# Pre-norm attention and GEGLU block on one core: first steps on token chunk 0, and ScalarE's extra work spaced by a backlog count

## The chip, the cores and the metric

The kernel runs on one core of a Trainium2 chip. The metric is the device time of one execution in microseconds (us). PE is TensorE (PEld its weight loads), DVE is VectorE, ACT is ScalarE, POOL is GpSimd and SP is SyncE, which issues the DMAs.

## The reference

```python
B, S, D, H, F = 1, 2048, 512, 32, 1792           # bf16, Dh = 16
def attn(x):                                      # wqkv: D x 3D, wo: D x D
    q, k, v = split_heads(x @ wqkv)
    p = softmax(einsum("bhqd,bhkd->bhqk", q, k) * Dh ** -0.5)
    return merge_heads(einsum("bhqk,bhkd->bhqd", p, v)) @ wo
def ffn(x):
    return (gelu_tanh(x @ w_gate) * (x @ w_up)) @ w_down
h  = x + attn(layernorm(x))                       # no scale or shift, eps 1e-5
h2 = h + ffn(layernorm(h))                        # the result
```

## The kernel before

**Planner.** The Python code walks through the whole program and appends instructions to one list per engine (PE, ACT, DVE, POOL, SP) with `P.op` and `P.dma`. It derives the semaphore waits from the buffers that each reads and writes. Every engine works off its list strictly in order, so an instruction that waits holds up all that was appended to the same engine behind it. This also goes for SP: its DMAs wait in line.

**Start (lines 327 to 388).** The 2048 tokens are 16 tiles of 128, or 4 chunks of 512. DMAs load `x_sb` by chunks, then `wqkv_sb` in one piece, then `wo_sb`. `ln1_stats(c)` takes mean and variance of a chunk's tiles on DVE (lines 351, 352), and POOL turns them into `rstd` and `nmr1` with a power (lines 355 to 358). `ln1_norm` writes the normalized `xn_sb` on DVE for chunks 0 to 2 and on POOL for chunk 3 (line 362); PE transposes each tile with four matmuls (line 367), and ACT copies the result from PSUM to `xnT` (line 369). `w_order` reorders the K and Q weights on DVE (line 374). Then `dense.run_items(5)` projects K for all four chunks and Q for chunk 0 of the first head group (`item_projT`, line 564); ACT writes them with their masks straight from PSUM (`direct`, lines 591 and 593).

**Heads.** Eight slots of four heads each; a head has 16 channels in a 32-row strip. One K or Q projection (`ht`) gives two slots: the even one by a masked copy, and the odd one from a copy `QKS` which a DMA shifts by 16 partitions into one of two `QKS2` buffers (line 597), which POOL then masks (`mask_emit`, lines 584 and 586). `qk_late` holds the copies of the five first projections, whose shifts come just ahead of step 0.

**Steps (loop at the end, "ticks").** The queries are 8 groups (`gi`) of 256; a unit is one group and one slot, 64 units of 16 steps, 1024 steps. In each step pass 1 computes two score tiles (line 666) of 512 keys, and DVE takes their row maxima (`TENSOR_REDUCE`, line 675). POOL combines them, SP transposes them by DMA (line 715), and POOL adds them to Q (line 720). Pass 2 follows 24 steps later: PE computes the transposed scores with the maximum subtracted (line 736, two tiles a step), and ACT takes two exponentials of 128 x 512 (line 748) into a ring `PTM`, `PTE`, `PTG`. The four PSUM banks 4 to 7 hold pass 2's tiles and one item of the dense stream.

**Dense stream.** `Dense` is a queue of generators. A call of `dense.piece()` emits some four matmuls, and each step calls it once; before pass 2 has begun, twice. Items: K, Q and V projections (`item_projT`, `item_projV`, line 616), `item_pv` (probabilities times V, line 762, evacuated into `OA`), `item_ofin` (transposes, evacuated into `OAT`), `item_oproj` (ACT sums `xres` and squares it into `OnT`, lines 875 and 882), `item_gate` and `item_up` (line 942, evacuated into `g_sb` and `u_sb`), `item_down` (line 990). Where a step has less than two pieces, `dummy` fills it with matmuls that nobody reads (line 1148). `startable` says whether the item at the head may begin.

**ScalarE's extras.** `evac_act` (line 529) is ACT's copy out of PSUM. The tanh of the GELU (line 925, in `gelu_chain.later`) and the squares (line 882, `sq`) are put off by a step while the set `act_extra` holds this step or the one before:

```python
if not force[0] and (dense.now in act_extra or (n < 3 and (dense.now - 1) in act_extra)):
    defer(1, lambda: later(n + 1))
    return
act_extra.add(dense.now)
```

The evacuations of gate, up, OA, OAT and the projections do not ask.

**End.** Behind the last step pass 2 runs out, and the last group's output projection, layer norm and feed-forward follow (`tail_b`). With `gi` the index of a query group, the last one is `GL` = 7; it uses ACT's own GELU (line 955).

## Time and profile before

| what | value |
|---|---|
| median of 3 runs (lowest, highest) | 1288.84 us (1288.76, 1289.89) |
| the profiled execution's own time | 1289.83 us |
| its span, first to last instruction | 1287.7 us |
| busy: PE, DVE, ACT, POOL | 91%, 94%, 93%, 59% |
| DVE row maxima (line 675) | 1024, busy 1174.2 us |
| ACT exponentials (line 748) | 1388 + 420 + 240 |
| HBM over the span | 11 GB/s |

Lines of the profile name source line, engine, operation, tile written and tiles read, and shapes; then the count, the busy time, the mean length of one, and the idle time before them with what ended it. Instructions on one engine overlap a little, so the distance of two starts can be shorter than the length of one.

### The profile page before, as it was taken

How to read it: one execution, taken by the hardware profiler on the slowest of the kernel's cores; microseconds unless marked ns; L12 is line 12 of the kernel's file. 1: busy time of each engine (PE TensorE's matmuls, PEld its weight loads, DVE VectorE, ACT ScalarE, POOL GpSimd, SP SyncE). 2: the span in 40 equal slices, each digit the busy share in tenths (PEclk: the TensorE clock that was granted, in tenths of full speed). 3: DMA queues.
4: the chain of work that ended last, by engine and by line, in shares of the span. 5: the costliest groups of instructions: out<-in, count | busy, mean ns of one | idle time of the engine just before them, and what ended most of it. 6: DMA issues, size and time to landing. Idle time of an engine off the chain costs nothing.

```text
span 1287.7 us, 31480 instructions
## 1 busy us (share of the span) xinstructions
PE 1175.5 (91%) x12702; PEld 411.7 (32%) x12702; DVE 1205.1 (94%) x1104; ACT 1201.3 (93%) x2438; POOL 759.9 (59%) x1523
## 2 busy tenths in 40 slices
PE   3999988899999999999999999989999999999998
PEld 2222222233323332233323333233322333233335
DVE  5899999999999999999999999999999999999913
ACT  3599999999999999999999999999999999999992
POOL 5567763477635774467733876367744777347840
PEclk9999999999999999999999999999999999999999
DMA  3110003300010000100001000100001000100000
GB/s 131 42 32 23 21 20 118 88 6 5 4 30 13 6 4 9 29 11 3 6 22 20 6 6 5 28 14 6 6 8 34 5 4 6 30 14 4 5 12 17
DMA packets 48688, 27.45 MB, mean 21 GB/s; under 512 B 34976, under 2 KB 47008, under 8 KB 48544
## 3 DMA queue, kind: packets, MB, share of 16 engines
q1 hardware_dynamic: 48544, 25.44, 7.6%
q8 instruction: 101, 1.65, 0.5%
q14 instruction: 43, 0.35, 0.1%
HBM read 11.80 MB, written 2.10 MB: 11 GB/s over the span
## 4 chain that ended last, share of the span: by engine, by line
ACT 48%; PE 37%; DVE 11%; issue 2%; POOL 0%; DMA 0%
ACT PTM L748 27%; PE pbank L762 10%; DVE PM L675 10%; ACT PTG L748 8%; PE pbank L1148 6%; PE pbank L666 6%; PE pbank L736 5%; ACT PTE L748 5%; PE pbank L990 5%; ACT th_sb L925 2%; ACT g_sb L529 1%; PE pbank L616 1%; ACT OA L529 1%; ACT u_sb L529 1%; PE pbank L564 1%
## 5 line engine op out<-in xcount | busy, mean ns | idle before, releaser
L675 DVE TENSOR_REDUCE PM<-pbank 128x2 f32<-128x1024 f32 x1024 | 1174.2, 1215 | 29.8 <-PE pbank L666 14.1
L748 ACT ACTIVATE PTM<-pbank 128x512 bf16<-128x512 f32 x1388 | 741.9, 655 | 17.8 <-PE pbank L736 8.4
L736 PE MATMUL pbank<-QT,KT 32*128 32x256 bf16 x4096 | 492.2, 273 | 3.4
L666 PE MATMUL pbank<-KT,QT 32*128 32x512 bf16 x2048 | 397.6, 384 | 9.5 <-DVE PM L675 5.4
L1148 PE MATMUL pbank<-ones_bf,ident 128*128 128x512 bf16 x846 | 261.5, 384 | 39.9 <-ACT u_sb L529 8.3
L748 ACT ACTIVATE PTG<-pbank 128x512 bf16<-128x512 f32 x420 | 228.8, 645 | 4.2 <-PE pbank L736 1.9
L666 PEld LDWEIGHTS pbank<-KT,QT 32*128 32x128 bf16 x2048 | 97.6, 91 | 346.8 <-DVE PM L675 135.9
L736 PEld LDWEIGHTS pbank<-QT,KT 32*128 32x128 bf16 x4096 | 165.2, 92 | 53.6 <-ACT PTM L748 22.2
L762 PE MATMUL pbank<-PTM,VA 128*17 128x256 bf16 x2776 | 154.9, 275 | 14.9 <-PE pbank L762 0.2
L748 ACT ACTIVATE PTE<-pbank 128x512 bf16<-128x512 f32 x240 | 137.4, 653 | 3.1 <-PE pbank L736 1.4
L701 POOL TENSOR_TENSOR MX<-PM,MX 128x8 f32<-128x8 f32 x64 | 12.9, 201 | 170.2 <-DVE PM L675 170.2
L1148 PEld LDWEIGHTS pbank<-ones_bf,ident 128*128 128x128 bf16 x846 | 51.5, 97 | 151.3 <-ACT PTM L748 90.7
L797 POOL TENSOR_TENSOR LINV<-OAT,negone 128x16 f32<-128x16 f32 (+1 forms) x32 | 92.7, 2898 | 7.6 <-DVE OAT L518 7.6
L762 PEld LDWEIGHTS pbank<-PTM,VA 128*17 128x17 bf16 x2776 | 42.7, 87 | 107.5 <-PE pbank L762 75.6
L942 PE MATMUL pbank<-hnT_l,wu_sb 128*128 128x256 bf16 x448 | 67.1, 275 | 5.0 <-ACT PTG L748 0.2
L942 PE MATMUL pbank<-hnT_l,wg_sb 128*128 128x256 bf16 x448 | 67.0, 275 | 4.3 <-ACT PTG L748 0.6
L690 POOL TENSOR_TENSOR MX<-PM,MX 128x8 f32<-128x8 f32 x64 | 13.0, 204 | 97.5 <-DVE PM L675 97.5
L934 POOL TENSOR_TENSOR th_sb<-th_sb,g_sb 128x512 f32<-128x512 f32 x49 | 62.2, 1269 | 4.1
L931 POOL TENSOR_TENSOR th_sb<-th_sb,g_sb 128x512 f32<-128x512 f32 x49 | 62.1, 1267 | 2.9
L983 POOL TENSOR_TENSOR GUT<-th_sb,u_sb 128x512 bf16<-128x512 f32 x49 | 62.2, 1268 | 2.7
L990 PE MATMUL pbank<-wd_sb,GUT 128*128 128x512 bf16 x224 | 60.5, 382 | 3.5
L720 POOL TENSOR_TENSOR QT<-QT,STG 128x256 bf16<-128x256 bf16 x64 | 42.8, 669 | 34.0 <-DMA STG<-ST 33.9
(128 smaller groups left out, 1069.9 us busy)
## 6 DMA issues: line engine op xcount, KB each, us to landing
QKS<-QKS SPq DMA_DIRECT2D x32, 112.0 KB, 2.1
x_sb<-in_A_x_dram SPq DMA_DIRECT2D x4, 512.0 KB, 5.5
xres<-in_A_x_dram SPq DMA_DIRECT2D x16, 128.0 KB, 2.2
out_dram<-out_sb SPq DMA_DIRECT2D x16, 128.0 KB, 1.7
wg_sb<-in_B_w_gate_dram SPq DMA_DIRECT2D x4, 448.0 KB, 4.9
wu_sb<-in_B_w_up_dram SPq DMA_DIRECT2D x4, 448.0 KB, 4.8
wqkv_sb<-in_A_wqkv_dram SPq DMA_DIRECT2D x1, 1536.0 KB, 10.3
wd_sb<-in_B_w_down_dram SPq DMA_DIRECT2D x3, 512.0 KB, 6.5
```

Of the source, the lines that this page charges most:

```text
L666: P.op("pe", lambda e, g=g, b=b: e.matmul(pbank[:, b, :], QT[32 * g:32 * g + 32, c, slot, 128 * qt:128 * qt + 128], KT[32 * g:32 * g + 32, ...
L675: P.op("dve", lambda e: e.tensor_reduce(out=PM[:, par, qt, kc, g:g + 2], in_=pbank[:, b:b + 2, :], axis=AX.X, op=ALU.max), reads=[("pb", b ...
L736: P.op("pe", lambda e, kt=kt, i=i: e.matmul(pbank[:, b, 256 * i:256 * i + 256], KT[32 * g:32 * g + 32, slot, 128 * kt:128 * kt + 128], QT[ ...
L748: P.op("act", lambda e, b=b, pi=pi: e.activation(out=PTt(pi), in_=pbank[:, b, :], func=ACT.Exp), reads=[("pb", b)], writes=[("PT", pi)], e ...
L762: P.op("pe", lambda e, g=g, kt=kt, pi=pi, i=i: e.matmul(pbank[32 * g:32 * g + 17, b, 0:256], VA[:, kt, 4 * slot + g, :], PTt(pi)[:, 256 * ...
L797: P.op("pool", lambda e: e.tensor_tensor(out=li, in0=oat4[:, :, :, 16], in1=negone[:, 0:8 * ns].rearrange("p (q h) -> p q h", q=2), op=ALU ...
L931: o(1.27, lambda e: e.tensor_tensor(out=ts_, in0=ts_, in1=gs, op=ALU.mult), [("th", par), ("g", par)])], then=done)
L934: o(1.27, lambda e: e.tensor_tensor(out=ts_, in0=ts_, in1=gs, op=ALU.mult), [("th", par), ("g", par)])], then=lambda: defer(TANH_LAG, lamb ...
L942: P.op("pe", lambda e, dc=dc, fc=fc, i=i: e.matmul(pbank[:, b, 256 * i:256 * i + 256], w[:, dc, 128 * fc:128 * fc + 128], hT[:, dc, :], st ...
L983: P.op("pool", lambda e: e.tensor_tensor(out=o_ap, in0=shp(ts_), in1=shp(us), op=ALU.mult), reads=[("th", par), ("u", par)], writes=o_keys ...
L990: P.op("pe", lambda e: e.matmul(pbank[:, b, :], GUT[:, fc, 128 * k:128 * k + 128], wd_sb[:, fc, :], start=(fc == 0), stop=False), reads=[( ...
L1148: P.op("pe", lambda e: e.matmul(pbank[:, b, :], ident[:], ones_bf[:, 0:512], start=True, stop=True), reads=["ident", "ones_bf"], writes=[( ...
```

## The change

- **Start.** The K and Q weights are loaded as a piece of their own ahead of V's. The layer norm is done tile by tile: statistics on DVE (`stats_dve`) or on ACT (`stats_act`: a copy and a square, each with an accumulated sum; tiles 4 to 6, 11 and 14). Chunk 0 is transposed on PE as before; the tiles of chunks 1 to 3 are transposed by DMAs on SP (`xnT_dma`). The weights are reordered by head group, the first on DVE, the others on ACT beside the steps. Only K and Q of chunk 0 are projected ahead of step 0. The norm of chunk 3, its transposes, the statistics of tiles 12 to 15 and the other K chunks of the first head group come at given steps (`early`) or as items of the dense stream; those K items write their even slot at once (`at_once`).
- **Steps before pass 2.** The second `dense.piece()` is left out in every fourth step. `dummy` takes a bank that the current item does not use.
- **Warm-up.** 16 and 3 filler matmuls at the start (`warm`).
- **Spacing.** The set `act_extra` becomes a number, `act_lag`. Each extra adds its cost in us, and each step takes off 1.135 less 0.478 per exponential. Tanh and squares wait while it is above 0.2 (tanh: plus 0.1 for each step that it has waited). Gate and up items start only at 0.4 or below. A gate item starts only when its buffer is free or the next item with a set time is at least 10 steps off; the first down item of a group starts only when the group's products are all issued, instead of waiting 7 steps with the bank in hand.
- **End.** The choice of the GELU goes by `gi == GL`.

The diff, cut to its core:

```diff
+LAG_START = 0.4
+LAG_OP = 0.2
...
-        P.dma("sp", lambda e: e.dma_start(out=wqkv_sb[:], in_=wv), "wqkv", writes=["wqkv"])
+        P.dma("sp", lambda e: e.dma_start(out=wqkv_sb[:, :, 0:2 * D], in_=wv[:, :, 0:2 * D]), "wqk", writes=["wqk"])
+        P.dma("sp", lambda e: e.dma_start(out=wqkv_sb[:, :, 2 * D:3 * D], in_=wv[:, :, 2 * D:3 * D]), "wqkv", writes=["wqkv"])
...
-        ln1_stats(0)
-        ln1_stats(1)
-        ln1_norm(0, "dve")
-        ln1_stats(2)
-        ln1_norm(1, "dve")
-        ln1_stats(3)
-        ln1_norm(2, "dve")
-        w_order(wk_r, D, "wk_r")
-        ln1_norm(3, "pool")
-        w_order(wq_r, 0, "wq_r")
...
+        def xnT_dma(t):
+            P.dma("sp", lambda e: e.dma_start_transpose(out=xnT[:, :, 128 * t:128 * t + 128], in_=xn_sb[:, t, :]), ("xnT", t), reads=[("xn", t)], writes=[("xnT", t)])
...
+        def warm(n):
+            for _ in range(n):
+                P.op("pe", lambda e: e.matmul(pbank[:, 0, :], ident[:], ones_bf[:, 0:512], start=True, stop=True), reads=["ident", "ones_bf"], writes=[("pb", 0)], sig=False)
+
+        warm(16)
+        for t in range(4):
+            stats_dve(t)
+        rstd_bn(0, 4)
+        rstd_pow(0, 4)
+        for t in range(4, 7):
+            stats_act(t)
+        stats_dve(7)
+        stats_dve(8)
+        rstd_sums(4, 7)
+        rstd_bn(7, 8)
+        rstd_pow(4, 8)
+        for t in range(4):
+            norm1(t, "dve")
+            xnT_pe(t, 4 + t)
+        warm(3)
+        stats_dve(9)
+        w_order("k", 0, "dve")
+        w_order("q", 0, "dve")
+        stats_act(11)
+        stats_dve(10)
+        rstd_bn(8, 11)
+        rstd_sums(11, 12)
+        rstd_pow(8, 12)
+        nmr(8, 12)
+        for t in range(8, 12):
+            norm1(t, "pool")
+
+        def c3_rest():
+            rstd_bn(12, 14)
+            rstd_sums(14, 15)
+            rstd_bn(15, 16)
+            rstd_pow(12, 16)
+            nmr(12, 16)
+            for t in range(12, 16):
+                norm1(t, "pool")
...
-        def startable(it):
+        def startable(it, room):
+            if it[0] is item_gate and par_busy[it[1][1] % 2] and room < 10:
+                return False
+            if it[0] is item_down and it[1][1] == 0 and not force[0]:
+                return not gut_left.get(it[1][0], 0) and dense.now >= gut_last.get(it[1][0], 0) + 1
...
-                        elif self.ready and (not self.single or (startable(self.ready[0]) and ...
+                        elif self.ready and (not self.single or ((act_lag[0] <= LAG_START or force[0] or self.ready[0][0] not in (item_gate, item_up)) and startable(self.ready[0], lim - self.now) and ...
...
-        act_extra = set()
+        act_lag = [0.0]
+        def act_more(cost):
+            act_lag[0] += cost
+        def act_tick(exps):
+            act_lag[0] = max(0.0, act_lag[0] + 0.478 * exps - 1.135)
...
+        k0 = [(item_projT, "k", 0, c, True) for c in range(1, NCH)]
+        qkv_items = [(item_projT, "k", 0, 0), (item_projT, "q", 0, 0), vs[0], vs[1], k0[0], vs[2], vs[3], k0[1], vs[4], vs[5], k0[2]]
+        vs = vs[6:]
+        for it in kq[:5]:
+            qkv_items += [it, vs.pop(0)]
+        qkv_items += vs + kq[5:]
...
-        dense.run_items(5)
+        dense.run_items(2)
         p1_begun[0] = True
-        for fn_ in qk_late:
-            fn_()
-        dense.banks = [7, 4, 5, 6]
+        for t in range(4, 8):
+            norm1(t, "dve")
+            xnT_dma(t)
+        for t in range(8, 12):
+            xnT_dma(t)
+        dense.banks, dense.rr = [6, 7, 4, 5], 0
+        early = {0: qk_late + [lambda: stats_act(14), lambda: stats_dve(12)], 1: [lambda: stats_dve(13)], 2: [lambda: stats_dve(15), c3_rest, lambda: w_order("k", 1, "act")],
+                 6: [lambda: [xnT_dma(t) for t in range(12, 16)]],
+                 5: [lambda: w_order("q", 1, "act")], 7: [lambda: w_order("k", 2, "act")], 9: [lambda: w_order("q", 2, "act")],
+                 11: [lambda: w_order("k", 3, "act")], 13: [lambda: w_order("q", 3, "act")]}
...
             def sq():
-                if not force[0] and ((dense.now in act_extra) or ((dense.now - 1) in act_extra and dense.now - 1 != sq_t0[0])):
+                if not force[0] and act_lag[0] > LAG_OP:
...
             def later(n):
-                if not force[0] and (dense.now in act_extra or (n < 3 and (dense.now - 1) in act_extra)):
+                if not force[0] and act_lag[0] > LAG_OP + 0.1 * n:
                     defer(1, lambda: later(n + 1))
                     return
-                act_extra.add(dense.now)
+                act_more(0.54)
...
         def item_down(b, gi, k):
-            if k == 0:
-                yield ("wait", 7)
             while gut_left.get(gi, 0):
                 yield ("wait", 1)
...
             dense.tick(tick)
+            act_tick(2 * p2_ok)
...
             cost = dense.piece()
-            if cost and not p2_started:
+            if cost and not p2_started and tick % 4 != 3:
                 dense.piece()
+            for fn_ in early.get(tick, ()):
+                fn_()
             want = 2 if p1_ok else 3
             if (cost or 0) < want:
-                dummy(banks.free[0], want - (cost or 0))
+                dummy(next(b for b in banks.free if dense.gen is None or b != dense.bank), want - (cost or 0))
```

More of the change, by code (lines that the diff above doesn't have):

```diff
@@ new lines, in xnT_pe @@
+        def xnT_pe(t, b):
+            pt = pbank[:, b, :].bitcast(BF16)
+            for dc in range(4):
+                P.op("pe", lambda e, dc=dc: e.transpose(out=pt[:, 128 * dc:128 * dc + 128], in_=xn_sb[:, t, 128 * dc:128 * dc + 128], identity=ident[:]),
+                     reads=[("xn", t), "ident"], writes=[("pb", b)], sig=(dc == 3))
+            P.op("act", lambda e: e.activation(out=xnT[:, :, 128 * t:128 * t + 128], in_=pt[:, 0:512].rearrange("p (c s) -> p c s", c=4), func=ACT.Copy),
+                 reads=[("pb", b)], writes=[("xnT", t)])
@@ L521, in evac_act @@
                 return
-            act_extra.add(dense.now)
+            act_more(cost)
             kw = {}
@@ L574, in dst, with direct @@
                 return KT[:, slot, 512 * c:512 * c + 512], [("kT", slot, c)]
+            def direct():
+                o_ap, keys = dst(2 * ht)
+                if which == "q":
+                    P.op("act", lambda e: e.activation(out=o_ap, in_=pbank[:, b, :], func=ACT.Copy, scale=qmask[:, 0:1]), reads=[("pb", b), "qmask"], writes=keys)
+                elif not p1_begun[0]:
+                    P.op("dve", lambda e: e.tensor_scalar(out=o_ap, in0=pbank[:, b, :], scalar1=kmask[:, 0:1], scalar2=kbias[:, 0:1], op0=ALU.mult, op1=ALU.add), reads=[("pb", b), "kmask", "kbias"], writes=keys)
+                else:
+                    P.op("act", lambda e: e.activation(out=o_ap, in_=pbank[:, b, :], func=ACT.Identity, bias=kbias[:, 0:1], scale=kmask[:, 0:1]), reads=[("pb", b), "kmask", "kbias"], writes=keys)
+            if at_once:
+                direct()
+            si, s2 = qk_n[0] % 4, qk_n[0] % 2; qk_n[0] += 1
+            while qks_busy.get(("a", si)) or qks_busy.get(("b", s2)):
+                yield ("wait", 1)
             def mask_op(src, key, slot, bk):
```

118 lines of the change are left out of this document (57 added, 61 removed).

## The prediction

> **What bounds the kernel now.** I read the groups of the page first, then the stages by windows, then the timeline of the start and of one stalled stretch.
>
> ```profile
> span 1287.7 us, 31480 instructions
> L675 DVE TENSOR_REDUCE PM<-pbank 128x2 f32<-128x1024 f32 x1024 | 1174.2, 1215 | 29.8 <-PE pbank L666 14.1
> ```
>
> One group carries the span: 1024 maximum reductions on VectorE, one per step, busy for 91% of it. So I cut the span at the starts of reductions 1, 25, 81, 177, 257 and 385, and at the last end, 1227.15.
>
> ```profile
> 0.00:34.32 34.32, 13.96 (x86) 8.44 (x86) 18.17 (x56) 14.15 (x24) 16.55 (x32) 1.00 0.36 123
> 34.32:67.96 33.64, 32.61 (x149) 10.04 (x150) 29.39 (x24) 16.05 (x29) 20.53 (x34) 0.95 0.15 44
> 67.96:131.70 63.74, 60.07 (x620) 17.91 (x619) 63.66 (x57) 63.15 (x130) 43.58 (x78) 1.00 0.10 28
> 131.70:240.30 108.60, 97.14 (x1112) 28.31 (x1112) 108.60 (x98) 105.95 (x212) 57.22 (x112) 1.00 0.23 68
> 334.15:482.97 148.82, 138.15 (x1550) 47.99 (x1549) 146.71 (x129) 145.84 (x300) 90.20 (x186) 1.00 0.05 12
> 1227.15:1287.72 60.57, 56.36 (x474) 26.92 (x471) 12.78 (x25) 34.30 (x63) 14.69 (x20) 1.00 0.05 15
> ```
>
> Columns: stage, its length, then busy time (instructions) of PE, PEld, DVE, ACT, POOL, then clock, DMA share, GB/s. Steps 80 to 175 run without a gap: 108.60 / 96 = 1.131 us, the floor of a step. Three losses stand above it. Before step 0 lie 34.32 us. The first 24 steps take 33.64 us, 6.5 over their floor of 27.1, with PE busy 97%. From step 176 the feed-forward work runs beside attention: the 128 steps from 334.15 take 148.82 us, 4.0 over 144.8. Between step 176 (240.30) and the last reduction's start (1.21 before 1227.15, 847 steps on) 985.6 us pass, 27.6 over the floor. The 60.57 us behind the last reduction have a PE that is nearly full.
>
> What makes the 4.0 shows in one stretch:
>
> ```profile
> 416.87 1.08 ACT L748 ACTIVATE PTG<-pbank 128x512 bf16<-128x512 f32 x2
> 417.84 0.63 ACT L925 ACTIVATE th_sb<-th_sb 128x512 f32<-128x512 f32 x1
> 418.36 1.09 ACT L748 ACTIVATE PTG<-pbank 128x512 bf16<-128x512 f32 x2
> 419.31 0.41 ACT L529 ACTIVATE OA<-pbank 128x256 f32<-128x256 f32 x1
> 419.58 2.10 ACT L748 ACTIVATE PTM<-pbank 128x512 bf16<-128x512 f32 x4
> 421.49 0.68 ACT L529 ACTIVATE u_sb<-pbank 128x512 f32<-128x512 f32 x1
> 420.47 2.36 DVE L675 TENSOR_REDUCE PM<-pbank 128x2 f32<-128x1024 f32 x2 [0.17 <-PE pbank L736]
> 423.19 6.97 DVE L675 TENSOR_REDUCE PM<-pbank 128x2 f32<-128x1024 f32 x6 [0.36 <-PE pbank L736]
> ```
>
> ScalarE owes two exponentials a step: 419.58 to 421.49 holds four, 0.478 each. That leaves 1.131 - 0.956 = 0.175 a step for the extras: tanh 0.52 (417.84 to 418.36), OA 0.27, u 0.48. Three of them within four steps put the exponentials late, a PSUM bank comes free late, PE stops at L736, and VectorE idles. The extras fit on average (ACT 145.84 of 148.82); their bunching costs.
>
> **The start, followed in order.** It is the larger rewrite.
>
> ```profile
> 2.94 0.75 SPq L330 DMA_DIRECT2D wqkv_sb<-in_A_wqkv_dram  x1
> 4.87 0.69 DVE L351 BATCH_NORM_STATS2 stats<-x_sb 128x6 f32<-128x512 bf16 x1 [2.32 <-DMA x_sb<-in_A_x_dram]
> 5.70 0.66 DVE L351 BATCH_NORM_STATS2 stats<-x_sb 128x6 f32<-128x512 bf16 x1
> 6.49 0.66 DVE L351 BATCH_NORM_STATS2 stats<-x_sb 128x6 f32<-128x512 bf16 x1
> 8.57 1.04 POOL L356 TENSOR_TENSOR rstd<-rstd,nhalf 128x4 f32<-128x4 f32 x1
> 11.25 1.35 DVE L362 TENSOR_SCALAR xn_sb<-x_sb,rstd,nmr 128x512 bf16<-128x512 bf16 x4
> 12.33 2.06 ACT L369 ACTIVATE xnT<-pbank 128x512 bf16<-128x512 bf16 x4 [10.27 <-PE pbank L367]
> 20.73 2.46 POOL L356 TENSOR_TENSOR rstd<-rstd,nhalf 128x4 f32<-128x4 f32 x1
> 21.45 0.89 DVE L374 COPY wk_r<-wqkv_sb 128x512 bf16<-128x512 bf16 x4
> 23.90 3.04 POOL L362 TENSOR_SCALAR xn_sb<-x_sb,rstd,nmr 128x512 bf16<-128x512 bf16 x4
> 27.64 4.61 PE L564 MATMUL pbank<-xnT,wk_r 128*128 128x512 bf16 x16
> 32.08 1.03 PE L564 MATMUL pbank<-xnT,wq_r 128*128 128x512 bf16 x4
> 33.15 0.69 ACT L591 ACTIVATE QT<-pbank,qmask 128x512 bf16<-128x512 f32 x1
> wqkv_sb<-in_A_wqkv_dram SPq DMA_DIRECT2D x1, 1536.0 KB, 10.3
> 390.05 0.78 ACT L882 ACTIVATE OnT<-xres 128x512 bf16<-128x512 bf16 x1
> 390.66 2.21 ACT L748 ACTIVATE PTM<-pbank 128x512 bf16<-128x512 f32 x4
> ```
>
> Today step 0 waits for the norm of all 16 tiles, GpSimd's four (23.90 to 26.9) the last, and for four K chunks. After the change it needs chunk 0. Its statistics start at 4.87 as now, 0.79 a tile (5.70 to 6.49); the power ends at 9.6. Two more tiles' statistics fit before that, so its norm starts at 9.7 instead of 11.25 and ends at 11.1. ScalarE's six sums cost 0.61 each (390.05 to 390.66), until about 10.1, then four copies into xnT, 2.06, end near 12.6. The weights landed at 13.2 (2.94 + 10.3); two thirds of them alone come about 1.4 earlier, 0.5 MB at the 370 GB/s which the loads run at, so 11.8. Two quarter-reorderings, some 0.5 in all by L374, are done by 12.6 too. K and Q are four matmuls each, 1.03 at full clock by the row at 32.08 and, I estimate, under 2 at half, which the first of the sixteen at 27.64 had; Q's copy is 0.69, the first score pair 0.4: **step 0 at about 16.5, bounds 15.6 to 17.4, instead of 34.32.** The 19 filler matmuls have no reader and run while PE waits for data; they cost nothing, and they decide between the two clocks.
>
> Those 17.8 are not all kept. Chunks 1 to 3 now arrive beside the steps, on queues that work in order:
>
> ```profile
> 35.00:40.00 5.00, 4.65 (x15) 1.32 (x16) 2.59 (x3) 2.47 (x5) 1.77 (x3) 0.66 0.31 91
> 36.82 1.23 DVE L675 TENSOR_REDUCE PM<-pbank 128x2 f32<-128x1024 f32 x1 [1.27 <-PE pbank L666]
> 39.18 1.22 DVE L675 TENSOR_REDUCE PM<-pbank 128x2 f32<-128x1024 f32 x1 [1.14 <-PE pbank L666]
> L848 SPq DMA_TRANSPOSE OnT<-Otok x14: 1189/1233/2034, 227.9 to 1121.9; - x14
> DMA to landing us min/median/max: 2.4/2.5/4.4
> L584 POOL TENSOR_SCALAR QT<-QKS,qmask 128x512 bf16<-128x512 bf16 x31 | 48.3, 1567 | 2.5 <-DMA QKS<-QKS 1.6 <-ACT QKS L529 0.9
> L586 POOL TENSOR_SCALAR KT<-QKS,kmask,kbias 128x512 bf16<-128x512 bf16 x28 | 21.5, 773 | 23.2 <-DMA QKS<-QKS 15.9 <-ACT QKS L529 7.3
> ```
>
> - VectorE takes three tiles' statistics between steps 0 and 3 (3 x 0.79 = 2.4) and chunk 1's norm (1.3) before step 0, beside Q's matmuls.
> - Tiles 4 to 15 are transposed by DMA: SP is held 1.24 for each, and a tile lands 2.5 after its issue. Chunk 1's four, issued from about 15.2, have landed at 21.5. PE meets K's chunk 1 behind pair 2, so step 3 starts near 23.4, about where VectorE comes from its statistics. Chunk 2 lands by 26.5: half a microsecond at step 7.
> - Chunk 3 is the place that binds. Tile 15's statistics leave VectorE at 22.4. GpSimd then does a power (1.04), small operations (1) and four norms (3.0) until 27.5, and only behind those the slot-1 masks of K (0.77) and Q (1.57), until 29.9. SP has the shift DMA of K's chunk 2 queued ahead of chunk 3's transposes; its buffer is the one that Q's mask reads. So the four transposes are issued from 30.5 and land at 36.7, where step 10 was due at 32. PE waits in front of pair 10, some 5 us, then runs at half clock as the row of 0.66 shows after a pause (steps of 2.5 and 2.36 there; two such steps cost 2.4). Step 12 starts near 42.8.
> - From there PE binds up to step 24. It takes 1.29 a step now (20 steps after the first slow ones); one piece of 0.43 less in every four steps gives 1.18: 12 x 1.18 = 14.2.
>
> Step 24 starts at 57.0 instead of 67.96: **gain 11.** Bounds: 17, if SP does not wait for that mask; 5, if the transposes land in 4.4 and GpSimd is held up as in the row at 20.73 (2.46 for 1.04). About six items of the projections move behind step 24, V's evacuations back to back among them; steps 24 to 79 had 0.4 over their floor (63.74 - 63.35). I put **1** lost there, 0 to 3, since four extra evacuations are 1.9 against 1.2 of slack.
>
> On the transposes a rule speaks against the change. The Trainium skill, "VectorE: DVE Perf Modes", The three transpose paths, prices a 128 x 128 transpose by DMA at 1309 ns and by TensorE at 390, and its rules prefer TensorE where a PSUM result will do. By its figure a 128 x 512 tile would be an estimated 5.2 us; the row's 2.5 for such a tile disagrees, and I go by the row.
>
> **The spacing.** Sorted by the starts of the reductions against the evacuations beside them (the two VectorE rows above, idle 0.17 and 0.36, are one each of the first two kinds), the 4.0 of one 128-step period are 1.3 where OA follows a tanh (five times), 1.05 where u follows those two, 0.55 at the output projection and its squares, 0.7 where a gate or up evacuation meets the PV matmuls, 0.2 at the outputs. The new count holds gate and up back above 0.4, tanh and squares above 0.2, so the second class goes, 0.9 of it; OA still waits for nobody and follows a tanh as before in about half of the places (0.65 gone); of the squares 0.3, of the gates 0.35. That is 2.2 of 4.0, or 55% of 27.6: **gain 15.** Bounds: 25, if all but the outputs goes; 2, if the delayed extras meet the next PV. The feed-forward may start its items later, but has room: of 0.175 a step OA takes 0.27 / 16, so seven blocks of g, u and tanh (1.48 each) need some 66 of the 128 steps. Removing the 7-step wait ahead of the down projection is free: its bank and its place in the stream come back earlier.
>
> **Sum.** The profiled run took 1289.83 for a span of 1287.7, 2.1 around it; the median of the runs is 1288.84, 1.0 below it. Span: 1287.7 - 11 + 1 - 15 = 1262.7; against the median, 1288.8 - 25 = **1264**. The end, 60.57, stays.
>
> **Rivals.**
> - *No convoy, nearly all bunching gone.* Start 17, spacing 22, 1 lost: 1251. For: SP's order depends on a mask of 1.57 alone. Against: GpSimd works in order. 0.18.
> - *The stalls only move.* PE is busy 138 of 149, so a delayed evacuation can meet PV's matmuls instead; spacing 2, start 11, 1 lost: 1277. 0.16.
> - *The feed-forward of one group spills behind the last step,* because held-back starts miss their places between two PVs.
>
> ```profile
> L942 PE MATMUL pbank<-hnT_l,wu_sb 128*128 128x256 bf16 x448 | 67.1, 275 | 5.0 <-ACT PTG L748 0.2
> ```
>
> An eighth of that is 8.4, as much again for the gate: 17 on a full PE, 1281. It decides where a block takes over 18 steps. For: a gate now also waits for the count. Against: the 66 steps above. 0.07.
> - *The transposes go one after another (slower).* At 4.4 a tile instead of 1.24, twelve of them from 15.2 end at 68, step 10 starts there instead of at 38, and step 24 near 87: 19 lost, 15 won, 1 lost: 1294. It decides from about 4 us a tile. For: the maximum of 4.4, and this trace has no twelve of them in a row. Against: the median of 2.5. 0.10, with what else could hold the twelve up as long.
>
> **How the numbers follow.** The forecast gets 0.46, the rivals what stands beside them. The range takes in all but the slower one and the far edges: 1247 to 1282. A measurement of this kernel can tell about 0.2%, 2.6 us, from no change; that strip lies between the spill and the slower case: 0.03. Faster 0.46 + 0.18 + 0.16 + 0.07 = 0.87, slower 0.10.
>
> **What would show it.** First reduction at 16 to 17; three bn statistics between the first reductions; a gap of about 5 ahead of reduction 11 put down to PE, PE's wait to the DMA of xnT, and a clock below 1 behind it; reduction 25 near 57; 128 steps in about 146.6; no u within two steps of OA behind a tanh; an end of 60 to 61. Wrong would be a step 0 after 20, a period still at 148.8, or matmuls of group 6 in the last 30 us beyond its down projection.

## The result, and the profile after

The changed kernel takes 1271.41 us (median; 1270.95 to 1272.65) against 1289.34 for the kernel before on the same chip: a ratio of 0.9862, 95% interval 0.9845 to 0.988. The gain is 17.9, where 25 was forecast. The profiled execution took 1270.95 for a span of 1269.2.

From the page of the kernel after, its span and the group of the row maxima (L756 now):

```profile
span 1269.2 us, 31210 instructions
L756 DVE TENSOR_REDUCE PM<-pbank 128x2 f32<-128x1024 f32 x1024 | 1166.9, 1218 | 22.3 <-PE pbank L747 13.4
```

The kernel after by windows, cut as before at the starts of reductions 1, 25, 81, 177, then the 128 steps from 256, then what lies behind the last reduction. Columns as in the prediction; the busy time of PE is too low here, since this trace lacks some of its matmuls (see below).

```profile
0.00:15.73 15.73, 9.78 (x46) 3.96 (x47) 10.64 (x32) 9.45 (x22) 10.41 (x26) 1.00 0.81 267
15.73:60.42 44.69, 34.59 (x133) 9.03 (x134) 30.90 (x31) 20.03 (x42) 26.57 (x50) 0.81 0.27 63
60.42:124.74 64.32, 58.52 (x609) 18.31 (x618) 63.99 (x58) 63.74 (x131) 32.91 (x74) 1.00 0.08 22
124.74:233.32 108.58, 95.50 (x1095) 29.57 (x1112) 108.58 (x97) 106.67 (x217) 71.44 (x122) 1.00 0.18 52
325.81:472.78 146.97, 134.34 (x1533) 48.19 (x1552) 145.75 (x129) 145.07 (x302) 91.30 (x187) 1.00 0.05 12
1207.24:1269.22 61.98, 56.04 (x474) 27.83 (x481) 14.07 (x28) 34.38 (x63) 20.64 (x26) 0.99 0.05 15
```

Against the stages before, in us of the two profiled spans:

| stage | before | after | gained | forecast |
|---|---|---|---|---|
| up to step 24 | 67.96 | 60.42 | 7.5 | 11 |
| steps 24 to 79 | 63.74 | 64.32 | -0.6 | -1 |
| steps 80 to 175 | 108.60 | 108.58 | 0.0 | 0 |
| step 176 to the last reduction's end | 986.85 | 973.92 | 12.9 | 15 |
| end | 60.57 | 61.98 | -1.4 | 0 |

Step 0 indeed starts 18.6 earlier (15.73), but 11 of these are gone by step 24. Above its floor of 144.8 (128 times 108.60 / 96), the 128-step period fell from 4.02 to 2.18 in the first full period and about 2.07 in the others.

The start, in lines of the timeline of the kernel after (start, length, engine, line, operation, count, and in brackets the idle time ahead of it and what ended it):

```profile
12.63 1.02 PE L633 MATMUL pbank<-xnT,wk_r 128*128 128x512 bf16 x4 [0.63 <-DVE wq_r L408]
14.85 10.46 SPq L397 DMA_TRANSPOSE xnT<-xn_sb  x8
15.73 1.23 DVE L756 TENSOR_REDUCE PM<-pbank 128x2 f32<-128x1024 f32 x1
21.56 1.02 PE L633 MATMUL pbank<-xnT,wk_r 128*128 128x512 bf16 x4 [3.29 <-DMA xnT<-xn_sb]
23.16 2.36 DVE L756 TENSOR_REDUCE PM<-pbank 128x2 f32<-128x1024 f32 x2 [1.54 <-PE pbank L747]
23.77 3.04 POOL L382 TENSOR_SCALAR xn_sb<-x_sb,rstd,nmr 128x512 bf16<-128x512 bf16 x4
25.36 6.53 SPq L670 DMA_DIRECT2D QKS<-QKS  x4
28.43 1.58 POOL L663 TENSOR_SCALAR QT<-QKS,qmask 128x512 bf16<-128x512 bf16 x1
28.71 1.34 PE L633 MATMUL pbank<-xnT,wk_r 128*128 128x512 bf16 x4
30.76 0.59 ACT L598 ACTIVATE QKS<-pbank 128x512 bf16<-128x512 f32 x1
31.94 5.47 SPq L397 DMA_TRANSPOSE xnT<-xn_sb  x4
38.76 1.01 PE L633 MATMUL pbank<-xnT,wk_r 128*128 128x512 bf16 x2 [5.36 <-DMA xnT<-xn_sb]
40.35 1.23 DVE L756 TENSOR_REDUCE PM<-pbank 128x2 f32<-128x1024 f32 x1 [6.35 <-PE pbank L747]
```

This is the convoy of the prediction. POOL has finished chunk 3's norm at 26.8. SP nevertheless stands in the shift DMAs from 25.36 to 31.9. They wait for the buffers that POOL reads in its masks, in Q's until 30.01; the last of the four then still waits for its own data, the copy of K's chunk 2, which ACT writes from 30.76 to 31.35. Chunk 3's transposes are issued behind them, at 31.94, and PE idles for 5.4 ahead of pair 10.

In the steady part, the idle times of PE ahead of the filler matmuls by what ended them (the view of waits; the columns are total, times and longest), in the kernel before:

```profile
PE pbank L1148 <- ACT u_sb L529: 8.3, 14, 0.6
PE pbank L1148 <- ACT PTM L748: 7.6, 12, 0.6
```

The kernel after's own trace can't be used for this. It holds 669 of the fillers' matmuls but 823 of their weight loads, so 154 matmuls are missing, and the time in which they ran shows as idle:

```profile
L1227 PE MATMUL pbank<-ones_bf,ident 128*128 128x512 bf16 x669 | 214.7, 383 | 49.5 <-ACT PTM L829 23.6 <-ACT PTG L829 8.6 <-ACT PTE L829 3.8
L1227 PEld LDWEIGHTS pbank<-ones_bf,ident 128*128 128x128 bf16 x823 | 50.1, 97 | 129.3 <-ACT PTM L829 82.7 <-ACT PTG L829 28.5 <-ACT PTE L829 14.0
```

The trace of t3_early, a run below with the same spacing, holds all 823 of both:

```profile
PE pbank L1226 <- ACT PTM L828: 2.4, 4, 0.6
```

L1148, L1227 and L1226 are the fillers that nobody reads. Before, they stood in PE's queue waiting for the evacuation of u; that row is gone, and the waits for exponentials have become shorter. So before a total of waits is read, the number of matmuls is to be compared with that of their weight loads.

### The profile page after: what moved, and what is told of

It is laid out like the page before. It is cut to its first block, busy times and chain, and to the rows that moved or that the text cites. A ratio compares the mean times of both kernels' runs of the same rounds, so it can differ in the third digit from the quotient of the medians.

```text
span 1269.2 us, 31210 instructions
## 1 busy us (share of the span) xinstructions
PE 1138.7 (90%) x12471; PEld 403.8 (32%) x12650; DVE 1193.8 (94%) x1089; ACT 1194.9 (94%) x2455; POOL 763.5 (60%) x1536
## 4 chain that ended last, share of the span: by engine, by line
ACT 41%; DVE 27%; PE 26%; POOL 2%; issue 2%; DMA 1%; SPq 0%
DVE PM L756 27%; ACT PTM L829 23%; PE pbank L843 7%; ACT PTG L829 7%; PE pbank L747 5%; PE pbank L817 4%; ACT PTE L829 4%; PE pbank L1071 3%; PE pbank L1227 3%; ACT th_sb L1005 2%; ACT g_sb L598 1%; PE pbank L1022 1%; PE pbank L633 1%; PE pbank L689 1%; ACT OA L598 1%
## 5 line engine op out<-in xcount | busy, mean ns | idle before, releaser
L756 DVE TENSOR_REDUCE PM<-pbank 128x2 f32<-128x1024 f32 x1024 | 1166.9, 1218 | 22.3 <-PE pbank L747 13.4
L1227 PE MATMUL pbank<-ones_bf,ident 128*128 128x512 bf16 x669 | 214.7, 383 | 49.5 <-ACT PTM L829 23.6
L747 PEld LDWEIGHTS pbank<-KT,QT 32*128 32x128 bf16 x2048 | 101.1, 91 | 361.0 <-DVE PM L756 167.5
L817 PEld LDWEIGHTS pbank<-QT,KT 32*128 32x128 bf16 x4096 | 159.6, 92 | 56.1 <-ACT PTM L829 28.2
L782 POOL TENSOR_TENSOR MX<-PM,MX 128x8 f32<-128x8 f32 x64 | 12.9, 202 | 162.8 <-DVE PM L756 162.8
L1227 PEld LDWEIGHTS pbank<-ones_bf,ident 128*128 128x128 bf16 x823 | 50.1, 97 | 129.3 <-ACT PTM L829 82.7
L1012 POOL TENSOR_TENSOR th_sb<-g_sb 128x512 f32<-128x512 f32 x49 | 51.0, 1041 | 21.9 <-ACT g_sb L598 21.9
L843 PE MATMUL pbank<-PTG,VA 128*17 128x256 bf16 x840 | 59.0, 275 | 3.5
```

What stands on the lines that cost most here:

```text
L747: P.op("pe", lambda e, g=g, b=b: e.matmul(pbank[:, b, :], QT[32 * g:32 * g + 32, c, slot, 128 * qt:128 * qt + 128], KT[32 * g:32 * g + 32, ...
L756: P.op("dve", lambda e: e.tensor_reduce(out=PM[:, par, qt, kc, g:g + 2], in_=pbank[:, b:b + 2, :], axis=AX.X, op=ALU.max), reads=[("pb", b ...
L817: P.op("pe", lambda e, kt=kt, i=i: e.matmul(pbank[:, b, 256 * i:256 * i + 256], KT[32 * g:32 * g + 32, slot, 128 * kt:128 * kt + 128], QT[ ...
L843: P.op("pe", lambda e, g=g, kt=kt, pi=pi, i=i: e.matmul(pbank[32 * g:32 * g + 17, b, 0:256], VA[:, kt, 4 * slot + g, :], PTt(pi)[:, 256 * ...
L1012: pool.add([o(1.04, lambda e: e.tensor_tensor(out=ts_, in0=gs, in1=gs, op=ALU.mult), [("g", par)], dE), o(0.62, lambda e: e.tensor_scalar( ...
L1227: P.op("pe", lambda e: e.matmul(pbank[:, b, :], ident[:], ones_bf[:, 0:512], start=True, stop=True), reads=["ident", "ones_bf"], writes=[( ...
```

## Experiments

Each was run against the kernel before. "Period" is the excess of 128 steps over 144.8, taken from the starts of the row maxima; "end" is what lies behind the last of them.

| kernel | median us (lowest, highest) | ratio to before (95%) | step 0 | step 10 | step 24 | period | end |
|---|---|---|---|---|---|---|---|
| after | 1271.41 (1270.95, 1272.65) | 0.9862 (0.9845, 0.988) | 15.73 | 40.35 | 60.42 | 2.07 | 61.98 |
| spacing_only | 1276.67 (1276.48, 1277.94) | 0.9903 (0.9888, 0.9918) | 35.22 | 49.26 | 67.32 | 2.07 | 61.58 |
| old_count | 1278.97 (1276.42, 1281.06) | 0.9918 (0.9902, 0.9934) | 15.75 | 40.38 | 59.19 | 3.14 | 60.81 |
| t3_early | 1264.31 (1263.26, 1264.64) | 0.9803 (0.9786, 0.9819) | 16.63 | 36.55 | 53.97 | 2.07 | 61.96 |
| no_warm | 1271.12 (1270.08, 1272.21) | 0.9858 (0.9843, 0.9873) | 17.53 | 41.26 | 59.61 | 2.08 | 61.97 |
| t3_pe | 1264.76 (1264.33, 1265.97) | 0.9807 (0.9793, 0.9822) | 15.79 | 35.91 | 53.33 | 2.06 to 2.64 | 61.74 |
| tanh_pv | 1284.34 (1281.24, 1285.76) | 0.9954 (0.9939, 0.997) | 15.79 | 40.13 | 60.29 | 2.27 | 70.85 |
| starts_only | 1288.75 (1286.08, 1290.04) | 0.9989 (0.9979, 0.9999) | 16.05 | 40.59 | 62.45 | 2.78 to 3.63 | 72.94 |
| ops_only | 1278.60 (1277.15, 1280.99) | 0.9915 (0.99, 0.993) | 16.36 | 40.97 | 59.79 | 3.14 to 3.63 | 60.78 |
| before_room | 1286.63 (1285.98, 1288.07) | 0.9981 (0.9972, 0.9991) | 35.30 | 49.34 | 67.40 | 3.58 | 60.57 |
| no_room | 1271.54 (1270.04, 1274.53) | 0.9865 (0.9846, 0.9885) | 16.19 | 40.84 | 61.05 | 2.06 to 2.23 | 62.32 |
| t3_start05 | 1268.14 (1267.43, 1269.19) | 0.9837 (0.9822, 0.9851) | 15.83 | 34.94 | 52.36 | 3.00 | 60.67 |
| t1_pe | 1264.23 (1263.28, 1264.82) | 0.9805 (0.9788, 0.9823) | 16.74 | 36.25 | 53.67 | 2.05 to 2.36 | 61.74 |

(Periods are those from the second full one on. The first is higher in several runs: 4.02 in old_count, 3.4 in t3_pe, starts_only, t3_start05 and t1_pe, 2.83 in tanh_pv. Steps and ends are those of one profiled execution each: with the same start, step 0 lies between 15.73 and 16.74 in them.)

### The spacing alone: spacing_only

The kernel before with the count, the start rules and `est=5`, its own start kept:

```diff
+LAG_START = 0.4
+LAG_OP = 0.2
-        def startable(it):
+        def startable(it, room):
+            if it[0] is item_gate and par_busy[it[1][1] % 2] and room < 10:
+                return False
...
-        act_extra = set()
+        act_lag = [0.0]
...
-            if k == 0:
-                yield ("wait", 7)
```

> The kernel before with the spacing part alone (count, start rule, queue rules), its old start kept. Theory A (start and spacing are independent): step 0 at 34.3, step 24 at 68, a period of 128 steps in 146.9 instead of 148.8, the end some 1.4 longer: about 1277. Theory B (the spacing's gain hangs on the new order of the projections or on the later begin of the feed-forward): the period stays near 148.8 and the time above 1285.

It gains 12.6 of the median, with step 24 where the kernel before has it and the period of the kernel after. The end of spacing_only by windows:

```profile
35.22:67.32 32.10, 31.07 (x149) 9.81 (x150) 29.39 (x24) 16.05 (x29) 20.42 (x34) 1.00 0.16 46
1212.90:1274.48 61.58, 57.29 (x482) 27.83 (x481) 14.07 (x27) 34.37 (x63) 20.60 (x26) 1.00 0.05 15
```

From step 176 to the end of the last reduction it takes 973.2, and the kernel after 973.9: the spacing's gain doesn't hang on the new start. The start alone was not run; its share is what is left, 5.3 of 17.9. The longer end belongs to the spacing.

### The count undone: old_count

The kernel after with the sets of before in place of the count, the other rules kept:

```diff
-                if not force[0] and act_lag[0] > LAG_OP + 0.1 * n:
+                if not force[0] and (dense.now in act_extra or (n < 3 and (dense.now - 1) in act_extra)):
...
-                if not force[0] and act_lag[0] > LAG_OP:
+                if not force[0] and ((dense.now in act_extra) or ((dense.now - 1) in act_extra and dense.now - 1 != sq_t0[0])):
```

(`act_lag` stays at 0, so no threshold holds gate and up items back.)

> The changed kernel with the count undone: tanh and squares ask the old set again, gate and up start without a threshold; the rules for the gate's buffer and the first down item stay. Theory A (the count carries the gain): period back near 148.8, an end of 60.6, about 1283. Theory B (the queue rules carry it): period still near 147, about 1270 to 1272.

The period is 3.14, between the two: the queue rules (gate's buffer, down without its 7-step wait, the filler's bank) carry 0.88 of it and the count 1.07. In the first full period it is still 4.02. Over the whole stage from step 176 to the last reduction's end, 986.85 before, it takes 981.65, against 973.92 with the count: 5.2 for the queue rules and 7.7 for the count. Beside the count the filler's bank has no part: spacing_only lacks that rule and has the same 2.07 as the kernel after. The end is 60.81, so the longer end comes with the count.

### Chunk 3's transposes ahead of the shifts: t3_early

```diff
-        early = {0: ..., 2: [lambda: stats_dve(15), c3_rest, lambda: w_order("k", 1, "act")],
-                 6: [lambda: [xnT_dma(t) for t in range(12, 16)]],
+        early = {0: ..., 2: [lambda: stats_dve(15), c3_rest, lambda: [xnT_dma(t) for t in range(12, 16)], lambda: w_order("k", 1, "act")],
```

> The changed kernel with chunk 3's four transposes put on SP's queue at step 2, ahead of the shift DMAs of K's chunks 1 and 2 (now at step 6, behind them). Theory A (SP's wait for the slot-1 masks makes the gap ahead of step 10): the transposes are issued from about 26.4 and land by 33; step 10 at about 34.7 instead of 40.35, less of the half clock behind it, step 24 at 53 to 55 instead of 60.4: 1264 to 1266. Theory B (the masks, which now come later, hold up steps 16 to 28, or the chain through GpSimd is as long): step 24 near 59, about 1270.

It takes 7.1 less than the kernel after, by order in one queue alone, as the first theory had it. The timeline of t3_early:

```profile
26.17 1.25 SPq L670 DMA_DIRECT2D QKS<-QKS  x2
27.46 5.22 SPq L397 DMA_TRANSPOSE xnT<-xn_sb  x4
32.80 6.97 SPq L670 DMA_DIRECT2D QKS<-QKS  x4
35.59 0.59 PE L633 MATMUL pbank<-xnT,wk_r 128*128 128x512 bf16 x2 [0.24 <-DMA xnT<-xn_sb]
```

and its windows from step 0 to step 24:

```profile
16.63:53.97 37.34, 32.98 (x136) 8.87 (x134) 30.74 (x31) 20.06 (x42) 25.80 (x48) 0.86 0.38 76
```

The transposes are issued at 27.46 instead of 31.94, PE waits 0.24 instead of 5.36, and the second stretch at half clock is gone. Step 24 comes 6.5 earlier, and the rest of the run keeps that.

### Without the filler matmuls: no_warm

```diff
-        warm(16)
...
-        warm(3)
```

> The changed kernel without the 19 filler matmuls. Theory A (they buy the full clock for the first transposes and projections): a clock below 1 until step 0, step 0 some 1.5 to 2 later, and all behind it as much: about 1273. Theory B (the half clock in steps 3 to 9 comes anyway and the chain through SP decides): step 10 unmoved, 1271.4.

The first K and Q in the timeline of no_warm, with the first reduction:

```profile
12.93 1.87 PE L631 MATMUL pbank<-xnT,wk_r 128*128 128x512 bf16 x4 [0.97 <-ACT xnT L393]
14.59 1.74 PE L631 MATMUL pbank<-xnT,wq_r 128*128 128x512 bf16 x4
17.53 1.22 DVE L754 TENSOR_REDUCE PM<-pbank 128x2 f32<-128x1024 f32 x1 [0.60 <-PE pbank L745]
```

K and Q take 1.87 and 1.74 here, 1.02 and 1.03 with the fillers, and step 0 is 1.8 later; step 24 is not later at all (59.61 against 60.42). (The windows view shows a clock of 1.00 there, but the trace has no clock on record ahead of 16.01; the lengths show the half clock.) The fillers don't always hold the clock either: in t3_early, which has them, it was at half from 11.1 to 14.5, K took 1.86, and step 0 came at 16.63. Chunk 3's transposes bind behind all of this. So the fillers moved step 0 by 0.8 to 1.8 and, as long as the convoy stands, nothing else. Whether they are worth something in t3_early was not tried.

### Chunk 3 transposed on PE: t3_pe

Two items of eight transposes ahead of K's chunk 3, copied by ACT; no DMA transposes for tiles 12 to 15:

```diff
-        qkv_items = [..., k0[1], vs[4], vs[5], k0[2]]
+        qkv_items = [..., k0[1], vs[4], (item_xnT2, 12), (item_xnT2, 14), k0[2], vs[5]]
...
-                 6: [lambda: [xnT_dma(t) for t in range(12, 16)]],
```

> The changed kernel with chunk 3 transposed on PE (two dense items of eight transposes each, ScalarE copies them to xnT) instead of by four DMAs on SP. Theory A (the gap ahead of step 10 is SP's order): no wait on a DMA there, step 10 at 33 to 34 instead of 40.35, no half clock behind it, step 24 near 51 to 52, the rest as in the changed kernel: 1262 to 1263, and 2 below the kernel that only puts the transposes first. Theory B (the norm of chunk 3 on GpSimd is late, whoever transposes): step 10 at 37 or later, 1266.

Timeline of t3_pe:

```profile
32.13 0.61 PE L711 MATMUL pbank<-ident,xn_sb 128*128 128x128 bf16 x8
32.83 2.06 ACT L715 ACTIVATE xnT<-pbank 128x512 bf16<-128x512 bf16 x4
33.00 0.62 PE L711 MATMUL pbank<-ident,xn_sb 128*128 128x128 bf16 x8
34.95 0.60 PE L633 MATMUL pbank<-xnT,wk_r 128*128 128x512 bf16 x2 [1.33 <-ACT xnT L715]
```

As fast as t3_early, no faster. Four tiles take 2.8 here, from 32.13 to the end of the copies at 34.89; by DMA in t3_early they hold SP for 5.2, and a tile lands 2.5 behind its issue in the median, but they begin 4.7 earlier. The Trainium skill ("VectorE: DVE Perf Modes", Rules for kernel authors) prefers TensorE where a PSUM result will do. For four tiles in a row the trace agrees on the length, and shows that it does not decide here: the PE items stand in the order of the steps, and steps 3 to 6 ran at half clock (23.1 to 29.9). The periods of t3_pe scatter between 2.06 and 2.64 with the same order of items; why stays open.

### Tanh kept away from the steps that hold PV: tanh_pv

```diff
-                if not force[0] and act_lag[0] > LAG_OP + 0.1 * n:
+                if not force[0] and (act_lag[0] > LAG_OP + 0.1 * n or 3 <= dense.now % 16 <= 8):
```

This was aimed at a stall in the kernel after, in its timeline:

```profile
422.84 0.92 ACT L1005 ACTIVATE th_sb<-th_sb 128x512 f32<-128x512 f32 x1
423.36 0.89 ACT L829 ACTIVATE PTM<-pbank 128x512 bf16<-128x512 f32 x1
424.30 0.11 PEld L817 LDWEIGHTS pbank<-QT,KT 32*128 32x128 bf16 x2 [0.58 <-ACT PTM L829]
425.85 3.49 DVE L756 TENSOR_REDUCE PM<-pbank 128x2 f32<-128x1024 f32 x3 [0.41 <-PE pbank L817]
```

A tanh put in while the PV item holds one of four banks delays an exponential, PE's transposed scores wait 0.58 for its bank, and the reductions lose 0.41.

> The changed kernel; a tanh is also put off in steps 3 to 8 of each 16, where the PV matmuls hold a bank. Theory A (what is left of the stalls is a tanh put in while PV holds one of the four banks): the period falls from 2.07 over its floor to about 1.0, 7 us in all, less up to 2 at the end, as the feed-forward ends later: 1265 to 1267. Theory B (the late tanh meets the next gate or OA instead): period at 2 or more, 1271 to 1274.

It takes 12.9 more than the kernel after, far from both theories. The period rose to 2.27, and the feed-forward of group 6 did not finish in time. The end of tanh_pv by windows, and the longest wait of its PE:

```profile
1208.66:1279.51 70.85, 60.23 (x489) 29.20 (x489) 14.07 (x28) 34.89 (x64) 20.70 (x26) 0.95 0.04 13
PE pbank L1071 <- POOL GUT L1064: 5.9, 1, 5.9
```

The theory that these stalls would simply go fell: by the starts of the row maxima they now lie at other places, among them two evacuations of gate or up two steps behind a tanh, 0.25 each. What the run prices instead is the late feed-forward: 8.9 at the end, of which 5.9 is that wait; behind it PE also works at half clock (0.50 from 1247.9 to 1254.7).

### One gate of the count at a time: starts_only and ops_only

```diff
-LAG_OP = 0.2
+LAG_OP = 99.0
```

> The changed kernel with the count asked only for the starts of gate and up; tanh and squares go when they are due. Theory A (the wait of tanh and squares is what spares OA): period at 3 to 4 over its floor instead of 2.07: 1277 to 1283. Theory B (the starts do the spacing): 2.0 to 2.5, 1271 to 1274.

```diff
-LAG_START = 0.4
+LAG_START = 99.0
```

> The changed kernel with the count asked only by tanh and squares; gate and up start without a threshold. Theory A (the starts keep u off OA, worth half of the count's 1.07): period at 2.5 to 2.7 over its floor, and the end back at 60.6 to 61: 1273 to 1274. Theory B (the starts do nothing but delay): period at 2.0 to 2.1, end shorter, 1270.

With the start threshold alone the period is 2.78, between the two theories, and the end, which neither of them touched, is 11.0 longer than in the kernel after:

```profile
1214.29:1287.23 72.94, 60.91 (x499) 29.81 (x497) 15.26 (x29) 34.90 (x64) 26.71 (x32) 0.95 0.04 13
PE pbank L1071 <- POOL GUT L1064: 6.9, 1, 6.9
```

In the order of the dense items, two up items of group 6 now stand behind the last step, and the down projection waits 6.9 for POOL's products. With the other threshold alone the period is 3.14 to 3.63, above both theories, and the end is that of before. So the start threshold carries about 1.1 of a period (3.14 to 2.07), and without it there is no longer end. The threshold on tanh and squares carries 0.7 (2.78 to 2.07), beside the other, against tanh and squares that never wait; without the other, it does no better than the old sets (3.14 in old_count).

### The gate's buffer rule, added and taken away: before_room and no_room

The rule put into the kernel before, and taken out of the kernel after:

```diff
             if it[0] is item_gate and par_busy[it[1][1] % 2] and room < 10:
                 return False
```

> The kernel before with one rule alone: a gate item whose buffer is busy starts only when the next item with a set time is 10 steps off (before, it started at once and kept its PSUM bank while it waited). Theory A (that bank is what the fillers lack: with three banks in turn they are put on the one from which u is still being copied, 14 waits of 0.6): these 14 waits go, the period falls by 0.88 over its floor to 3.14 as in the kernel without the count, nothing else moves: 1283.5. Theory B (the down rule or the filler's bank gave that part): period at 4.0, 1289.

> The changed kernel without that rule for the gate. Theory A (the bank matters wherever a gate waits for its buffer): waits of fillers for u come back, up to 0.88 a period, 1274 to 1277. Theory B (the count already keeps gates from starting that early): period at 2.07, 1271.4.

Alone it carries 0.44 of a period (4.02 to 3.58), half of what old_count gave the queue rules together, and halfway between the two theories; the rest was not taken apart. The weight loads of the fillers, complete in both traces, show the wait for u in the kernel before:

```profile
PEld pbank L1148 <- ACT u_sb L529: 12.2, 14, 0.9
```

In before_room no such row is left, as in the kernel after, and the period is still 3.58: those waits were at most 0.44 of it. (Of its fillers' matmuls the trace holds 684 of 846, so their own idle times can't be read.) In no_room the period is 2.06: beside the count the rule does nothing.

### A looser start threshold: t3_start05

t3_early with one more edit, to win back the end:

```diff
-LAG_START = 0.4
+LAG_START = 0.5
```

> The kernel with chunk 3's transposes first, and the threshold for gate and up at 0.5 instead of 0.4. By the planner's order this puts a whole feed-forward some 10 steps earlier: no up item of group 6 is left behind the last step, and the second output of a group stands 17 steps ahead of where it met the squares. Theory A: end 60.8 instead of 62.0; the stalls at the squares (0.8 a period) go: period at 1.3 to 1.6, 1259 to 1261. Theory B (gate and up closer together cost as much elsewhere): period at 2 to 2.5, 1263 to 1266.

The end is back at 60.67, but the period is 3.00, and the kernel takes 3.8 more than t3_early, above both theories. Tanh stood directly ahead of OA's evacuation again in five places of a period. A tenth of a microsecond in the threshold undoes half of the spacing's gain, and I can't say from these runs at which value it turns.

### Chunk 1 transposed on PE: t1_pe

t3_early, with the remaining wait of the start, 3.2 ahead of K's chunk 1, attacked:

```diff
-        qkv_items = [..., vs[0], vs[1], k0[0], vs[2], vs[3], k0[1], ...]
+        qkv_items = [..., vs[0], (item_xnT2, 4), (item_xnT2, 6), k0[0], vs[1], k0[1], vs[2], vs[3], ...]
...
             norm1(t, "dve")
-            xnT_dma(t)
```

> The version with chunk 3's transposes issued early (t3_early: median 1264.31, step 3 near 24, step 10 at 36.55, step 24 at 53.97), and chunk 1's four tiles transposed on PE beside step 1 instead of by DMA; K of chunk 1 and of chunk 2 come one place earlier in the list of projections. It asks whether PE's wait of some 3.2 us for chunk 1 and the stretch at half clock behind it are worth anything at step 24. Theory A, the wait costs itself and a part of the half clock: chunk 1's K at about 19.5, step 3 at 20 to 21, no half clock until the next wait, step 10 at 33 to 34, step 24 at 50.5 to 51.5, the median 1261 to 1262. Theory B, the chunks behind it bind just as late: the wait moves to chunk 2's transposes (issued behind GpSimd's norm, landing near 26) or chunk 3's, step 10 stays at 35.5 to 36.5 and step 24 at 53 to 54, the median 1263.5 to 1264.5. Periods (2.07) and the end (62) as in the version with early transposes in both.

The number is that of the second theory, but the reason is another. The timeline of t1_pe:

```profile
17.92 0.62 PE L709 MATMUL pbank<-ident,xn_sb 128*128 128x128 bf16 x8
19.91 0.63 ACT L358 ACTIVATE xn_sb<-x_sb 128x512 bf16<-128x512 bf16 x1
20.54 2.04 ACT L713 ACTIVATE xnT<-pbank 128x512 bf16<-128x512 bf16 x4
22.63 0.13 PEld L633 LDWEIGHTS pbank<-xnT,wk_r 128*128 128x128 bf16 x2 [3.07 <-ACT xnT L713]
```

PE had transposed the first two tiles by 18.5, but ACT's copies stood behind its two sums of tile 14 and began at 20.54. K's chunk 1 began at 22.63, PE had idled 3.07, and the clock went to half as before (21.4 to 31.7). The wait had only changed its owner. What its removal would bring stays open.

## Why the prediction was right, and where its terms were off

The sign, the likeliest case and the range (1247 to 1282) held. The forecast of 1264 is 7.4 too low. By stages: start 3.5 (11 forecast, 7.5 measured), steps 24 to 79 0.4 the other way (1 and 0.6), spacing 2.1 (15 and 12.9), the end 1.4 (0 and 1.4). That makes 6.6 of span (6.5 between the spans of 1262.7 and 1269.2); what is left lies between span and median.

- **Step 0** at 16.5 was right: 15.73, in the bounds. It came earlier as K and Q both ran at full clock, 1.02 and 1.03, where K was put under 2; that was in part luck, as t3_early's K, with the same start, took 1.86.
- **Step 3** at 23.4 was right (23.16), with its reason: PE waited 3.29 for chunk 1. The clock behind that wait was not in the sum. From 22.5 to 29.4 the clock stood at half, and steps 4, 5 and 6 took 2.15, 2.36 and 1.59.
- **The convoy** was the right mechanism, and t3_early shows it as a cause: only the order on SP changed, and the wait of 5.36 became 0.24. It was mis-sized twice. The transposes were issued at 31.94 instead of 30.5: Q's mask ended at 30.01, where the prediction had 29.9, but the wait that ended last was that of the shift of K's chunk 2 for its own copy, until 31.35, since K's chunk 2 had been projected at half clock (28.71 to 30.05). So K's chunk 3 began at 38.76 instead of 36.7. And half clock behind the gap was put at two steps, 2.4; it lasted until 46.4, and steps 10 to 12 took 2.49, 1.64 and 2.23. The bounds (5 to 17) held the 7.5.
- **Fillers.** "They decide between the two clocks" was right for step 0 between the kernel after and no_warm (1.8), though not in every execution with fillers (t3_early). For the time they decided nothing, because the convoy covers them. The prediction had the convoy and did not draw that.
- **Steps 24 to 79** lost 0.6, in the bounds of 0 to 3.
- **The spacing** was right in its independence (spacing_only) and nearly in its size: a period of 2.07 against 1.8. The classes, which add up to 3.8 of the 4.0, were less right. The second class was laid to the thresholds alone. old_count shows that the queue rules without the count already carry 0.88, and no_room that at least the gate's rule is no longer needed beside it; the causes overlap and can't be added class by class. Of the remaining 2.07, by the starts of the row maxima, 0.8 lie where group output copies and the squares fall beside the down projection, which was put at some 0.45; and 1.2 where a tanh falls on a PV item. That is not the 0.65 which was left for OA behind a tanh: OA still follows a tanh within four steps in five places of a period, and only one of its evacuations stands out (0.33).
- **"Removing the 7-step wait is free"** stands: nothing that had it removed showed a longer end by itself (old_count, 60.81 against 60.57).
- **The end** was the step that failed outright: "60.57 stays". By the order of the dense items one up item of group 6 stands behind the last step. In the timeline of the kernel after it appears 31.85 behind the last reduction, where DVE, done with its reductions, evacuates u:

```profile
1239.09 0.69 DVE L587 COPY u_sb<-pbank 128x512 f32<-128x512 f32 x1
```

  That is the spill rival in small. It was weighed as one block for all, spilled or not at all, and decided by the mean backlog (66 of 128 steps). It comes in single items, by the starts that the threshold holds back, and it is not their number that sets the price. One item costs 1.4 in the kernel after, where PE has no wait for POOL's products in the down projection. One, evacuated 40.0 behind the last reduction, costs 10.3 in tanh_pv (70.85 against 60.57), where PE waits 5.9 for them; two cost 12.4 in starts_only (72.94), with a wait of 6.9.
- **The rivals.** "No convoy" is what t3_early makes real: the start alone then gains 14.0 at step 24 (67.96 to 53.97), not 17; a wait of 3.20 for chunk 1 and the half clock behind it are still in that trace. "The stalls only move" is what happened in tanh_pv, not in this change. Transposes one after another did not come: eight held SP for 10.46, 1.31 each, and four for 5.47, where 1.24 each was forecast and 4.4 feared.
- **The transposes' path** was weighed with the Trainium skill's rule against the change, and the row of 2.5 a tile was preferred to the figure. t3_pe and t3_early, 1264.76 and 1264.31, show that for chunk 3 the path changes nothing once the queue's order is right.

## What to carry to other kernels

A start that is overlapped with the main loop is worth what the last-arriving piece allows, so follow each queue in its order, and put what the loop will wait for ahead of what itself waits for other engines; here one line moved in SP's order gave 7.1 us, more than the whole rewrite of the start had given (17.9 less the 12.6 of spacing_only, 5.3). Before sizing a threshold that holds work back, look at where that work ends: a gain in every period was partly paid back by single items that no longer fitted ahead of the last step. Stalls sorted by class tell where to look, but their prices don't add when several rules act on the same items; measure each rule both added to the old kernel and removed from the new one. The best versions here are t3_early, t1_pe and t3_pe, 1264.23 to 1264.76, which these runs don't tell apart.

## What the runs showed of the hardware

The granted clock stayed at half longer than PE's waits did. In the kernel after it changed at 22.53, 29.36, 36.18 and 46.42, which are two, two and three times 3.41 apart. Windows of 3.41 cut by these times, with the clock in the third column from the end:

```profile
22.53:25.94 3.41, 3.08 (x11) 0.71 (x10) 2.36 (x2) 1.90 (x5) 3.14 (x6) 0.50 0.56 114
25.94:29.36 3.42, 3.42 (x10) 0.82 (x9) 1.77 (x2) 1.66 (x4) 2.55 (x4) 0.50 0.24 69
39.60:43.01 3.41, 3.06 (x9) 0.78 (x10) 1.39 (x2) 1.26 (x2) 0.00 (x0) 0.50 0.00 0
43.01:46.42 3.41, 3.41 (x10) 0.64 (x8) 2.28 (x2) 1.33 (x4) 1.52 (x5) 0.50 0.24 70
```

and two of other runs, the first of old_count, the second of starts_only:

```profile
40.18:43.60 3.42, 3.29 (x10) 0.67 (x8) 1.96 (x2) 1.26 (x2) 0.00 (x0) 0.50 0.00 0
43.74:47.15 3.41, 3.41 (x10) 0.76 (x10) 1.86 (x3) 1.81 (x4) 2.01 (x6) 0.50 0.24 70
```

PE came back from its wait of 3.29 at 21.56. In the next window it still paused (3.08 of 3.41), in the one after not at all, and behind that one the clock was full; behind the wait of 5.36 it was the same, 3.06 and then 3.41. The Trainium skill ("TensorE: Matmul & The Clock Gate", Part 1) lets one busy window of about 3.4 us suffice for full clock. These stretches agree with it, if busy means without a pause. The other two rows don't fit one threshold: in old_count 3.29 of 3.42 was enough, and the clock was full from 43.60; in starts_only 3.41 of 3.41 was not, and it stayed at half until 50.56. So the length of a stretch at half clock can't be forecast from these traces: behind the second wait it ended at 43.6 in old_count, 46.4 in the kernel after and 50.6 in starts_only. What had looked like a wait of 3 to 5 us was thus followed by some 7 us of PE's work at half clock; in t3_early, with the second wait gone, the first stretch still ran from 21.4 to 31.6.
